# Head matmuls of an attention and feed-forward kernel: the constant 1.0 read with a step of zero in place of a tile of zeros, and fourteen of them in place of twelve

## Chip, core and metric

The kernel runs on one core of one Trainium2 chip. The metric is the device time of one execution in microseconds; the median of three runs of the kernel before is 176.75 us (176.69 to 177.01). Five engines work side by side and meet at semaphores: TensorE (PE; its weight loads have a row of their own, PEld), VectorE (DVE), ScalarE (ACT), GpSimd (POOL) and SyncE (SP), which here only issues transfers.

## What is computed

The reference is windowed attention with a few global keys and a distance bias for each head, followed by a feed-forward layer whose hidden value is the largest of three products:

```python
def _attn_ref(q, k, v, n_global, n_local):          # q, k, v: (4, 8, 768, 64)
    scores = scale * np.matmul(q, k.transpose(0, 1, 3, 2))
    rel = pos[:, None] - pos[None, :]
    is_global = pos[None, :] < int(n_global)         # 8
    is_local = (rel >= 0) & (rel < int(n_local))     # 96
    dist = np.where(is_global & ~is_local, float(n_local), np.abs(rel))
    scores = scores - slopes[:, None, None] * dist[None, :, :]
    scores = np.where(is_global | is_local, scores, -1000000000.0)
    a = np.exp(scores - np.max(scores, axis=-1, keepdims=True))
    a = a / (np.sum(a, axis=-1, keepdims=True) + 1e-09)
    return np.matmul(a, v)

def _moe_ref(x, w1, w2, w3, w_out):                  # x: (3072, 512), d_ff 768
    h = np.maximum(np.maximum(x @ w1, x @ w2), x @ w3)
    return h @ w_out
```

## The kernel before

The 3072 tokens are 24 tiles of 128 rows (four batches of six). For each pair of tiles q and k are loaded as float32, cast to bf16, transposed on TensorE into PSUM and copied to `qkT`. For each tile and each half of the heads (`u_S`) TensorE writes scores into a PSUM tile `sp`: for the first tiles it first adds the bias by two matmuls of 512 columns (L299), then the products of keys and queries (L306). ScalarE takes the exponential into `P` (L317), TensorE multiplies by v (L360), VectorE normalizes (L364 to L373), and the result is transposed into `xT`. The feed-forward layer takes chunks of 2 to 4 tiles: `u_F1` (L424) makes the hidden values, `u_F2` (L439) the output.

The order of the work is written out by hand in `SCHEDULE`: a string of units, each a letter and its numbers, issued one after the other to the engines' queues. Each engine takes its own instructions strictly in this order. The units that matter for this change are `D` (dummy matmuls), `c` (a cast of q or k), `x` (transposes with their copies), `B` and `K` (bias and mask tables of one head, made from the tile `rbq`), `S` (scores and exponentials), `C` and `W` (casts of v and of weights).

**The dummies.** `u_D(i, n)` issues n matmuls of 128x128 weights by 512 columns into a PSUM tile `wp` that nothing reads. A unit `D0.4` is `u_D(0, 4)`; a unit with n = 0 does nothing. Four dummies stand in each of D0, D4 and D5, ahead of anything else that TensorE does; D1.1 and D9.2 (three more) stand behind the first transposes, and D3.1 and D7.1 further on: 17 in all. `wp` takes a buffer of the pool `psH` with the tag "h", which has three and which the transposes' PSUM tiles use in turn, so a later dummy can wait until a copy has emptied a buffer.

**The head**, ahead of `SCHEDULE`. The first loads of k and q are issued from ScalarE's and SyncE's queues. GpSimd makes `dist` (iota, L513) and two selections of it (L520, L522) and a memset (L531) into `rbq`, then the identity `identb`. VectorE writes `shift` (L515, L516), then `zeros` (L518), the tile that the dummies read both as weights and as moving columns, then from `dist` by L524, L525, L527, L528, L529 and L530 the rest of `rbq`. ScalarE loads its table and runs one small activation (L517), and starts on the tables of `rbq` (L326 and L322) once L530 is done. On TensorE the first instruction is a dummy, which waits for the memset of `zeros`.

**The first real work on TensorE** is `x0.1.3`: the eight transposes of the first k (L282) from `qkp`, which VectorE casts (L188), and one copy to `qkT` by VectorE (L285). Then `x0.0.7`: sixteen small transposes of the first q (L261), copied by ScalarE (L268, two copies). D1.1 and D9.2 follow, then `S1.0.1`: two bias matmuls (L299) and eight products of keys and queries (L306) that need both the k copy and the q copies.

The program's preamble, ahead of all that, has GpSimd write a few constants, one value for each partition (L556 in the profile); behind it all engines meet at a barrier before their first instruction. One of these constants is 1.0 in bf16; in the kernel before nothing shown here reads it.

Of the kernel before, what the change touches and what calls it, by code (L numbers as in the profile page):

```python
# [13 lines left out]
BF16 = mybir.dt.bfloat16  # L14
# [8 lines left out]


SCHEDULE = """
    K7 l1.0 c1.0.2 K6 l1.1 B6.1 D0.4 D4.4 B5.1 D2.0 D5.4 K0 c0.1.1 c0.0.1 K2 D8.0 B0.1 B4.0 B1.0
    B3.0 x0.1.3 K1 K3 K5 c1.1.2 B7.0 x0.0.7 D1.1 D9.2 S1.0.1 Z0.1 B2.1 v0 C0.0.2 S1.1.1 G1.0 x1.0.8
    K4 M1.0 S0.0.1 M0.0 v1 x1.1.8 S2.1.1 S2.0.1 M2.0 C0.1.2 Y0.1.2 Y1.0.1 M1.1 V2.1 Y0.0.1 G2.1 A1.2
    S0.1.1 C1.0.2 C1.1.2 Y2.0.0 Y1.1.2 D3.1 S3.0.1 M3.0 M0.1 A0.2 S3.1.1 M3.1 l2.0 c2.0.2 x2.0.6
# [35 lines left out]
def kernel(  # L65
# [13 lines left out]
    nc = tc.nc  # L79
# [26 lines left out]
    persist = ctx.enter_context(tc.tile_pool(name="persist", bufs=1))  # L106
# [14 lines left out]

    identb = persist.tile([128, 128], BF16, name="identb")
    tiny = persist.tile([128, 1], FP32, name="tiny")
    zeros = persist.tile([128, 512], BF16, name="zeros")
    rbq = persist.tile([128, 3, 128], FP32, name="rbq")
    shift = persist.tile([128, 1], FP32, name="shift")
    far = persist.tile([128, 1], FP32, name="far")
# [18 lines left out]
    def heads(ap):  # L146
        return ap.rearrange("p (h e) -> p h e", e=65)
# [8 lines left out]
    def load_part(n, s):  # L156

        b, t0 = divmod(2 * n, NT)
        r = raw_pool.tile([128, 2 * DM], FP32, name="rawp", tag="raw")
        src = (q, k)[s][b, :, t0 * 128:(t0 + 2) * 128, :]  # L160
        if short_rows(n, s):
            r = r.rearrange("p (h x) -> p h x", h=H)
            dma = nc.scalar if (n, s) == (0, 1) else nc.sync
            dma.dma_start(out=r, in_=src.rearrange("h (i e) d -> i h (e d)", e=2))
        else:
            r = r.rearrange("p (z x) -> p z x", z=2)
            for z in range(2):
                nc.sync.dma_start(out=r[:, z], in_=src[4 * z:4 * z + 4].rearrange("h (i e) d -> i h (e d)", e=ET))
        raw["p", n, s] = r
# [328 lines left out]
    def u_D(i, n=0):  # L498
        if n == 0:
            return  # L500

        wp = psH.tile([128, 512], FP32, name="wp", tag="h")
        for _ in range(n):
            nc.tensor.matmul(wp, zeros[:, 0:128], zeros, start=True, stop=True)  # L504

    with tc.manual_schedule():
        load_part(0, 1)
        load_part(0, 0)

        BIGD = 60000.0  # L510
        dist = stage_pool.tile([128, 2, 2, 64], FP32, name="dist", tag="wst0")
        rtmp = stage_pool.tile([128, 128], FP32, name="rtmp", tag="wst0")
        nc.gpsimd.iota(dist, base=128, pattern=[[-1, 2], [1, 2], [2, 64]], channel_multiplier=-2,  # L513
                       allow_small_or_imprecise_dtypes=True)
        nc.vector.memset(shift[0:64], -128.0)  # L515
        nc.vector.memset(shift[64:128], -1.0)  # L516
        nc.scalar.activation(tiny, shift, AF.Exp, bias=0.0, scale=1.0)  # L517
        nc.vector.memset(zeros, 0.0)  # L518
        near, own = rbq[:, 0:2].rearrange("p s (e i) -> p s e i", e=2), rbq[:, 2]
        nc.gpsimd.affine_select(out=near, in_=dist, compare_op=ALU.is_ge, fill=BIGD, base=128,  # L520
                                pattern=[[-1, 2], [1, 2], [2, 64]], channel_multiplier=-2)
        nc.gpsimd.affine_select(out=near, in_=near, compare_op=ALU.is_ge, fill=BIGD, base=NL - 129,  # L522
                                pattern=[[1, 2], [-1, 2], [-2, 64]], channel_multiplier=2)
        nc.vector.tensor_scalar(out=own, in0=dist[:, 0].rearrange("p e i -> p (e i)"), scalar1=shift, scalar2=None, op0=ALU.add)  # L524
        nc.vector.memset(far, BIGD)  # L525
        for row in (0, 64):
            nc.vector.memset(far[row:row + NG // 2], float(NL))  # L527
        nc.vector.scalar_tensor_tensor(out=rtmp, in0=own, scalar=1.0 - NL, in1=own, op0=ALU.add, op1=ALU.mult)  # L528
        nc.vector.tensor_scalar(out=rtmp, in0=rtmp, scalar1=0.0, scalar2=far, op0=ALU.is_gt, op1=ALU.mult)  # L529
        nc.vector.scalar_tensor_tensor(out=own, in0=own, scalar=far, in1=rtmp, op0=ALU.min, op1=ALU.max)  # L530
        nc.gpsimd.memset(rbq[0:NG // 2, 0:2], float(NL))  # L531
        make_identity(nc, identb)
        for tvar in vo_first + vo_next + ve + vf:
            nc.vector.memset(heads(tvar)[:, :, 64:65], 1.0)

        units = {"l": load_part, "v": load_v, "c": cast_part, "x": u_x, "w": load_w, "o": load_wo, "C": cast_v,
                 "Y": u_Y, "Z": u_Z, "S": u_S, "M": u_M,
                 "A": u_A, "G": put_kg, "V": put_vg, "T": u_XT, "F": u_F1, "W": cast_w,
                 "K": u_K, "B": u_B, "Q": cast_wo, "O": u_F2, "E": u_E, "D": u_D}
        for u in SCHEDULE.split():  # L540
            units[u[0]](*(int(n) for n in u[1:].split(".") if n))
# [33 lines left out]
```

## Time and profile before

| | before |
|---|---|
| median of three runs | 176.75 us (176.69 to 177.01) |
| span of the profiled execution (its first to its last instruction) | 174.9 us |
| between them | 1.85 us |
| TensorE busy in the span | 169.3 us |
| VectorE, ScalarE, GpSimd busy | 132.5, 120.1, 14.3 us |
| granted TensorE clock, mean | 0.999 |

The profile is of one execution; its page gives its span, and no other time for that execution. What lies outside the span (launch, the end) is taken as the difference to the median, 1.85 us. A row of the timeline reads: start in us from the span's start, duration in us, engine, line of the kernel, operation, out<-in, shapes, how many instructions are merged; in brackets the idle time of the engine just before and what ended it. Matmuls are pipelined: each row lasts until its last result, so the durations of single matmuls overlap, and the pitch (start to start) is the cost of one in a row of them. A row of the windows gives busy time of TensorE, its weight loads, VectorE, ScalarE and GpSimd in a stretch, the granted clock, and what the transfers took and moved.

### The profile page before, as it was taken

The page shows a single profiled execution, that of the slowest core. Times are in us where ns is not written, and L with a number is a line of the kernel's source. Part 1 is how long each engine was busy: PE and PEld are TensorE (multiplying, and loading weights), DVE is VectorE, ACT ScalarE, POOL GpSimd, SP SyncE. Part 2 cuts the span into 40 slices and gives each one's busy share as a digit, 9 for nine tenths or more (in the row PEclk, how much of TensorE's full clock was granted, in tenths as well). Part 3 has the DMA queues.
Part 4 walks back from the last instruction along what each step waited for, and adds up shares of the span by engine and source line. Part 5 has one row for each costly group of instructions (what it writes and reads, how often), then busy time and mean ns, then how long its engine had stood idle before and what let it go on. Part 6 is the DMA issues. An engine that isn't in the chain of part 4 may idle for free.

```text
span 174.9 us, 4233 instructions
## 1 busy us (share of the span) xinstructions
PE 169.3 (97%) x1683; PEld 93.0 (53%) x1683; DVE 132.5 (76%) x288; ACT 120.1 (69%) x188; POOL 14.3 (8%) x25
## 2 busy tenths in 40 slices
PE   6999999999999999999999999999999999999992
PEld 2445654658684587754545545544455544444451
DVE  6668859889999999998978769995569873444510
ACT  6989999789988999999948977345594413121132
POOL 5269250000100000000000000000000000000000
PEclk9999999999999999999999999999999999999999
DMA  4999999999999999976999997563101750031205
GB/s 137 347 302 335 359 350 383 385 380 312 309 282 265 298 289 228 292 213 193 257 195 185 304 233 172 166 133 60 54 10 30 105 171 0 0 119 36 89 27 213
DMA packets 55507, 35.92 MB, mean 205 GB/s; under 512 B 18368, under 2 KB 47936, under 8 KB 55488
## 3 DMA queue, kind: packets, MB, share of 16 engines
q1 hardware_dynamic: 54304, 35.07, 73.9%
q10 hardware_dynamic: 1184, 0.59, 1.3%
q8 instruction: 13, 0.21, 0.5%
q14 instruction: 6, 0.05, 0.1%
HBM read 25.17 MB, written 6.29 MB: 180 GB/s over the span
## 4 chain that ended last, share of the span: by engine, by line
PE 94%; ACT 2%; DVE 1%; issue 1%; ACTq 0%; DVEq 0%
PE h L424 53%; PE po L439 18%; PE sp L306 7%; PE op L360 6%; PE wp L504 4%; PE tpr L261 2%; PE sp L299 2%; PE xtp L411 1%; ACT qkT L268 1%; ACT wo L496 1%; PE oph L360 1%; ACT P L317 1%; PE xtr L401 0%; PE tpp L282 0%; DVE qkT L285 0%
## 5 line engine op out<-in xcount | busy, mean ns | idle before, releaser
L424 PE MATMUL h<-xT,w 128*128 128x512 bf16 (+1 forms) x504 | 100.8, 349 | 0.0
L424 PEld LDWEIGHTS <-w 128*128 128x128 bf16 x504 | 46.7, 98 | 40.7 <-ACT w L493 0.6
L317 ACT ACTIVATE P<-sp 128x1024 bf16<-128x1024 f32 (+1 forms) x48 | 44.0, 956 | 9.2 <-PE sp L306 9.1
L429 ACT CAST h<-h 128x512 bf16<-128x512 f32 (+1 forms) x42 | 21.9, 531 | 22.1 <-PE h L424 22.1
L439 PE MATMUL po<-wo,ht 128*128 128x512 bf16 (+2 forms) x156 | 34.1, 363 | 0.0
L431 DVE TENSOR_TENSOR h<-h,h 128x512 bf16<-128x512 bf16 (+1 forms) x42 | 25.2, 605 | 10.9 <-PE h L424 8.9
L433 DVE TENSOR_TENSOR ht<-h,h 128x512 bf16<-128x512 bf16 (+1 forms) x42 | 25.5, 609 | 6.3 <-PE h L424 5.0
L334 DVE TENSOR_TENSOR P<-P,wmask 128x1024 bf16<-128x1024 bf16 x33 | 22.0, 684 | 2.0 <-ACT P L317 1.9
L439 PEld LDWEIGHTS <-ht 128*128 128x128 bf16 x156 | 14.3, 98 | 15.1 <-DVE ht L433 0.2
L448 ACT COPY ost<-po 128x512 f32<-128x512 f32 (+2 forms) x16 | 8.8, 553 | 15.8 <-PE po L439 15.3
L373 DVE TENSOR_TENSOR xb<-op,rz 128x512 bf16<-128x512 f32 x22 | 15.2, 692 | 0.8
L360 PEld LDWEIGHTS <-P 128*128 128x128 bf16 x352 | 13.4, 97 | 4.4 <-issue 0.7
L306 PE MATMUL sp<-qkT 64*128 64x128 bf16 x320 | 14.3, 218 | 0.1
L306 PEld LDWEIGHTS <-qkT 64*128 64x128 bf16 x320 | 9.3, 94 | 8.2 <-issue 5.1
L448 DVE COPY ost<-po 128x512 f32<-128x512 f32 (+1 forms) x10 | 6.5, 647 | 8.4 <-PE po L439 8.4
L188 DVE CAST qkp<-rawp 128x1024 bf16<-128x1024 f32 x12 | 8.2, 687 | 1.7 <-DMA rawp<-in_k_dram 1.6
L504 PE MATMUL wp<-zeros 128*128 128x512 bf16 x17 | 7.1, 559 | 1.5 <-DVE zeros L518 1.4
L188 ACT CAST qkp<-rawp 128x1024 bf16<-128x1024 f32 x8 | 8.4, 1050 | 0.0
L268 ACT COPY qkT<-tpr 128x512 bf16<-128x512 bf16 x12 | 6.6, 588 | 1.0 <-PE tpr L261 1.0
L268 DVE COPY qkT<-tpr 128x512 bf16<-128x512 bf16 x6 | 4.0, 688 | 3.9 <-PE tpr L261 3.9
L372 DVE RECIPROCAL rz<-op 128x8 f32<-128x8 f32 x22 | 4.4, 199 | 2.5 <-PE op L360 2.3
L360 PE MATMUL op<-vo,P 128*128 128x65 bf16 x128 | 5.4, 193 | 0.3 <-issue 0.3
(84 smaller groups left out, 127.9 us busy)
## 6 DMA issues: line engine op xcount, KB each, us to landing
rawv<-in_v_dram SPq DMA_DIRECT2D x12, 512.0 KB, 7.0
out_dram<-ost SPq DMA_DIRECT2D x23, 256.0 KB, 2.4
rawp<-in_k_dram SPq DMA_DIRECT2D x8, 512.0 KB, 5.9
rawp<-in_q_dram SPq DMA_DIRECT2D x12, 256.0 KB, 5.8
wst<-in_moe_w_dram SPq DMA_DIRECT2D x3, 1024.0 KB, 11.5
rawp<-in_q_dram SPq DMA_DIRECT2D x6, 512.0 KB, 6.2
wst<-in_moe_w_dram SPq DMA_DIRECT2D x3, 512.0 KB, 8.5
rawp<-in_k_dram SPq DMA_DIRECT2D x6, 256.0 KB, 8.6
```

The source lines that it names most:

```text
L188: copies[how](qk, src)
L306: nc.tensor.matmul(sp[:, z, i, ds], k_cols(T, hsl, jp, ds), q_cols(T, hsl, jp), start=not how, stop=True, skip_group_check=True)
L317: nc.scalar.activation(dst, src, AF.Exp, bias=0.0, scale=scale)
L334: nc.vector.tensor_mul(P, P, wmask[:, g, :, 0:2])
L360: nc.tensor.matmul(o, P[:, i, ds], vs[ds][:, h], start=(ds == 0), stop=(ds == len(vs) - 1), skip_group_check=True)
L373: nc.vector.tensor_tensor(out=x.rearrange("p (g h) d -> p g h d", g=2), in0=o4[:, :, :, 0:64], in1=rz[:, :, :, None].to_broadcast([128, 2, ...
L424: nc.tensor.matmul(ps, w123[f // 2][:, dm, j, (f % 2) * 128:(f % 2) * 128 + 128], xT[c][:, dm], start=(dm == order[0]), stop=(dm == order[ ...
L429: nc.scalar.copy(h01, ps)
L431: nc.vector.tensor_max(h01s[c, f], h01s[c, f], ps)
L433: nc.vector.tensor_max(ht[c][:, f], h01s[c, f], ps)
L439: nc.tensor.matmul(po, ht[c][:, f, tt * 128:(tt + 1) * 128], wo[:, f, cols], start=(f == 0), stop=(f == NF - 1))
L448: copy(ost, po)
```

## The change

- `zeros` is no longer allocated, and its memset on VectorE (L518) is gone.
- The dummies, all of them, read `ones`: the preamble's constant 1.0 in bf16, one element for each partition, presented as 128 x 512 with a step of zero along the columns. Both the weights and the moving columns are this view.
- D0.4 becomes D0.6: fourteen dummies ahead of the first transposes for twelve, 19 in all for 17.

```diff
-    K7 l1.0 c1.0.2 K6 l1.1 B6.1 D0.4 D4.4 B5.1 D2.0 D5.4 K0 c0.1.1 c0.0.1 K2 D8.0 B0.1 B4.0 B1.0
+    K7 l1.0 c1.0.2 K6 l1.1 B6.1 D0.6 D4.4 B5.1 D2.0 D5.4 K0 c0.1.1 c0.0.1 K2 D8.0 B0.1 B4.0 B1.0
...
-    zeros = persist.tile([128, 512], BF16, name="zeros")
+    ones = nc.const_aps.tensor(1.0, (128, 512), BF16)
...
-            nc.tensor.matmul(wp, zeros[:, 0:128], zeros, start=True, stop=True)
+            nc.tensor.matmul(wp, ones[:, 0:128], ones, start=True, stop=True)
...
-        nc.vector.memset(zeros, 0.0)
```

## The prediction

> **What bounds the kernel now.** I read the page first, then the windows by stage, then the chain of waits and the timeline of the head. The page:
>
> ```profile
> PE 169.3 (97%) x1683; PEld 93.0 (53%) x1683; DVE 132.5 (76%) x288; ACT 120.1 (69%) x188; POOL 14.3 (8%) x25
> PE 94%; ACT 2%; DVE 1%; issue 1%; ACTq 0%; DVEq 0%
> ```
>
> TensorE is busy for 97% of the span and makes 94% of the chain that ended last. The windows show where it is not (stretch and its length, busy us of PE, PEld, DVE, ACT, POOL, clock, transfers):
>
> ```profile
> 0.00:9.40 9.40, 7.85 (x43) 3.35 (x45) 6.18 (x26) 7.68 (x15) 3.30 (x11) 1.00 0.83 246
> ...
> 21.80:80.00 58.20, 58.15 (x724) 37.21 (x725) 53.59 (x119) 53.51 (x89) 3.02 (x3) 1.00 1.05 304
> 80.00:172.00 92.00, 91.49 (x691) 45.32 (x690) 62.93 (x118) 47.61 (x69) 0.00 (x0) 1.00 0.52 124
> ```
>
> From 21.8 us to 172 us TensorE idles 0.05 + 0.51 us. Whatever shifts the start of that stretch shifts the end by the same amount; nothing in it can soak up a gain or a delay. So the question is the head alone. The chain of waits through it (start, us, what):
>
> ```profile
> 1.07 0.28 DVE zeros L518
> ...
> 1.40 5.30 PE wp L504 x12
> 6.70 0.83 PE tpp L282 x8
> ...
> 7.56 0.70 DVE qkT L285
> ...
> 8.30 0.59 PE wp L504 x2
> 8.90 0.43 PE sp L299 x2
> ...
> 9.36 0.40 PE sp L306 x8
> ```
>
> Taken at its word, it says that the memset of the zeros and the dummies set the end. The timeline of TensorE and ScalarE at the same place says otherwise:
>
> ```profile
> 6.49 1.03 PE L282 MATMUL tpp<-identb,qkp 128*128 128x128 bf16 x8
> 7.45 0.41 PE L261 MATMUL tpr<-identb,qkp 64*128 64x64 bf16 x16
> 8.30 0.59 PE L504 MATMUL wp<-zeros 128*128 128x512 bf16 x2
> 8.73 0.59 PE L299 MATMUL sp<-bias,identb 128*128 128x512 bf16 x2
> 9.36 0.40 PE L306 MATMUL sp<-qkT 64*128 64x128 bf16 x8
> 3.11 2.10 ACT L326 ACTIVATE wmask<-rbq 128x384 bf16<-128x384 f32 x4 [0.43 <-DVE rbq L530]
> 5.12 1.33 ACT L322 ACTIVATE bias<-rbq 128x384 bf16<-128x384 f32 x3
> 6.36 1.59 ACT L326 ACTIVATE wmask<-rbq 128x384 bf16<-128x384 f32 x3
> 7.85 0.51 ACT L322 ACTIVATE bias<-rbq 128x384 bf16<-128x384 f32 x1
> 8.27 1.04 ACT L268 COPY qkT<-tpr 128x512 bf16<-128x512 bf16 x2
> ```
>
> Two 512-column matmuls in a row start 0.43 us apart as a pair (8.30 to 8.73), 0.215 us each. The two bias matmuls at 8.73 therefore free TensorE at 8.73 + 0.43 = 9.16, but the first products of keys and queries start at 9.36, 0.05 us after the second q copy ends on ScalarE (8.27 + 1.04 = 9.31). ScalarE has no gap back to 3.11, where it had waited for L530. **ScalarE's table work, not the dummies, releases the first products; TensorE's side has 9.36 - 9.16 = 0.20 us of slack.** The first exponential, and with it all that follows, hangs on this point.
>
> **The change, part by part.** First, when TensorE can start. The constant, and the first instructions after the preamble:
>
> ```profile
> 0.31 0.10 POOL L556 MEMSET const-bfloat16-1.0<- 128x1 bf16 x1
> 0.73 0.42 ACTq L164 DMA_DIRECT2D rawp<-in_k_dram  x1
> 0.80 0.06 DVE L515 MEMSET shift<- 64x1 f32 x1 [0.80 <-PEq L556]
> 0.83 0.36 POOL L513 IOTA dist<- 128x256 f32 x1 [0.39 <-POOLq L556]
> 1.07 0.27 DVE L518 MEMSET zeros<- 128x256 uint32 x1
> 1.40 5.30 PE L504 MATMUL wp<-zeros 128*128 128x512 bf16 x12 [1.40 <-DVE zeros L518]
> ```
>
> The constant is written by 0.41, ahead of the barrier, so a dummy has nothing left to wait for. Other engines' first instructions lie at 0.73 to 0.83; I take 0.77 for TensorE in place of 1.40, 0.63 us earlier.
>
> Second, how long the dummies hold it. Twelve run from 1.40 to the first transposes at 6.49: 5.09 us, 0.424 each, twice the 0.215 of the later pair. So TensorE is at half its pace here, and it changes between 6.49 and 8.30. (The granted clock of the first window is 1.00 and doesn't show this.) Two more cost 0.85. At this pace the fourteen end at 0.77 + 5.09 + 0.85 = 6.71, **0.22 us later than now** (0.18 to 0.28 for starts of 0.73 to 0.83): the earlier start is more than eaten by the two added. The row of the step-zero operand itself is missing from this trace. Its price lies between none, as the same shape from a full tile (0.424), and one pitch more for each matmul, if the read of one element again and again ran at half pace. I take none: the nearest row is the same matmul with another address pattern.
>
> Third, who notices 0.22 us. The data for the first transposes:
>
> ```profile
> 5.56 0.69 DVE L188 CAST qkp<-rawp 128x1024 bf16<-128x1024 f32 x1 [1.59 <-DMA rawp<-in_k_dram]
> 6.31 0.98 PEld L282 LDWEIGHTS <-qkp 128*128 128x128 bf16 x8 [0.52 <-DVE qkp L188]
> 7.02 0.35 DVE L322 TENSOR_SCALAR bias<-rbq 128x384 bf16<-128x384 f32 x1
> 7.56 0.69 DVE L285 COPY qkT<-tpp 128x1024 bf16<-128x1024 bf16 x1 [0.18 <-PE tpp L282]
> ```
>
> The cast ends at 6.25 and its weights load at 6.31, so the dummies already hold the transposes back by some 0.15 us. With 0.22 more, the k copy goes from 7.56 to 7.78, the pair of dummies that waits for its buffer from 8.30 to 8.52, the bias matmuls from 8.73 to 8.95, and TensorE is free at 9.38 for products that start at 9.36 now: the slack hides 0.20, and 0.02 us arrives. The q transposes end at 7.86 now and would at 8.08, ahead of the copy at 8.27. On VectorE the copy to `kf` and a bias table stand behind the k copy and end 0.22 later; their readers come after 9.69.
>
> The dummies may not stay at half pace until then: the pace changes with time, and work that starts 0.63 us earlier may reach the change earlier. If it falls before some 5.9 us (twelve dummies at 0.424 from 0.77 and two at 0.215 end at 6.29), the dummies are over when the cast has ended, the transposes start near 6.35 at a quarter of 0.215 each, and the k copy follows its neighbour on VectorE at 7.02 + 0.35 = 7.37, 0.19 earlier than now. Then TensorE is free for the products at 8.97, and ScalarE alone decides.
>
> The Trainium skill, page "TensorE: Matmul & The Clock Gate", Part 1, puts the change of pace at the end of a free-running window of some 3.4 us that was busy throughout. Before, that is 4.8 to 8.2 by the start at 1.40; the trace's change after 6.49 agrees. After, it would be 4.2 to 7.6, earlier than 5.9 in half of all executions.
>
> Fourth, what VectorE gains. The rows behind the memset, with GpSimd's beside them:
>
> ```profile
> 1.26 0.51 DVE L524 TENSOR_SCALAR rbq<-dist,shift 128x128 f32<-128x128 f32 x1
> 1.26 0.42 POOL L520 TENSOR_SCALAR_AFFINE_SELECT rbq<-dist 128x256 f32<-128x256 f32 x1
> 1.75 0.42 POOL L522 TENSOR_SCALAR_AFFINE_SELECT rbq<-rbq 128x256 f32<-128x256 f32 x1
> 2.00 0.31 DVE L528 SCALAR_TENSOR_TENSOR rtmp<-rbq 128x128 f32<-128x128 f32 x1
> 2.34 0.29 DVE L529 TENSOR_SCALAR rtmp<-rtmp,far 128x128 f32<-128x128 f32 x1
> ```
>
> L524 needs the iota, which ends at 0.83 + 0.36 = 1.19, and starts at 1.26 with L520, which needs it too: the memset (to 1.34) holds its start by little. But it lasts 0.51 where the same operation on the same shape, L529, lasts 0.29. So dropping the memset gives L530, and with it ScalarE's 3.11, between nothing and 0.22 us. I take 0.05: L524 ends at 1.77, 0.08 behind the end of L520 (1.68), as if it had waited for GpSimd rather than for the memset; L528 ends 0.14 behind L522.
>
> The Trainium skill, page "SBUF — State Buffer", section "Who interferes with whom", has VectorE and GpSimd share a port pair that the first to start holds to its end. By it L524 may win the pair once it is free to start a moment before L520; then L520 and L522 move back by some 0.2 us, L528 and L529 meet them instead, and the sum is again a gain of 0.05 to 0.1, no 0.22. No run here shows it yet.
>
> **The sum.** With an early change of pace: -0.05 from ScalarE's start, TensorE's side ahead of it. With a late one: +0.02. The one execution has the change 5.1 to 6.9 us behind the first dummy; as much behind 0.77 would be 5.9 to 7.7, at the border or late, but whether it follows the first dummy or the clock on the wall one trace doesn't tell. I take the early case; the other differs by 0.07 only. Between there and 21.8 us the gain could still be lost to a transfer that lands when it lands:
>
> ```profile
> 11.37 1.18 POOL L191 CAST vof<-rawv 128x512 bf16<-128x512 f32 x2 [0.77 <-DMA rawv<-in_v_dram]
> 13.86 0.33 PE L360 MATMUL oph<-vof,P 128*128 128x65 bf16 x5
> 21.64 0.26 PEld L424 LDWEIGHTS <-w 128*128 128x128 bf16 x2 [0.16 <-ACT w L493]
> ```
>
> The v cast waits for its transfer and ends at 12.55, but its reader comes at 13.86, 1.3 us later; the first weights wait for ScalarE, not for a transfer. So a small shift carries through. So I forecast 174.9 - 0.05 for the span, and with the 1.85 outside it 176.75 - 0.05 = **176.70 us**, no change that can be told. A measurement of this kernel tells about 0.2% from no change, 0.35 us.
>
> **The rivals.**
>
> *ScalarE's start moves in full.* If all that VectorE's steps lose to GpSimd goes, ScalarE could start when its first small activation is done (2.68) instead of 3.11; TensorE's side allows 9.36 - 8.97 = 0.39. That is the most the head can give: 176.36. For it: L524's 0.51 against 0.29. Against: the steps wait on GpSimd's, which do not get shorter.
>
> *TensorE doesn't start earlier.* The change then does not do what it says: something other than the memset (the load of its own instructions, the barrier) holds TensorE to its old start. The products come at its start + 5.94 for the fourteen + 2.67 (6.49 to 9.16), later than 9.36 if the start is later than 0.75, and over 0.35 us later from a start of 1.10. At 1.40 it costs 0.85 - 0.20 = 0.65: 177.40. Against: the wait named in the row at 1.40 is the memset's.
>
> *The pace falls back.* If the pace changes as early as 4.2, the dummies end at about 5.5 and TensorE idles until 6.3. If it then drops to half once more for as long as it takes to recover (some 3 us of matmuls from 9.4, less what hides under ScalarE), it costs about 1.5 us: 178.2. Against: idle stretches of 0.4 us at 8.3 and 9.3 leave the later pace alone, though they are shorter.
>
> *Step zero reads at half pace.* Fourteen dummies of 0.85 last 11.9 us, the transposes start at 12.7 for 6.49, less 0.20: 176.75 + 6.0 = 182.7. Nothing in the trace speaks for or against it.
>
> **How the numbers follow.** The forecast (with 0.02 late as its other half) 0.56, ScalarE's start in full 0.24, TensorE not earlier 0.12, the pace falls back 0.05, half pace reads 0.03. The forecast's own range is 176.5 to 176.95, its two ends with the spread of the three runs. To hold eight in ten I go down to the bound of the first rival, 176.3, and up to 177.1, half of the second rival; the slow two and the rest of the second stay out. Faster by over 0.35: 0.24. Slower: the two slow ones and the second rival's larger half with some room, 0.08 + 0.09 = 0.17. Within: 0.59.
>
> **What would show it.** In the profile after: the first dummy at 0.73 to 0.83 in place of 1.40 (else the second rival); fourteen at 0.424 up to 6.7, or at 0.215 from some point on; the first products within 0.1 us of 9.36 with the q copies of ScalarE ending just ahead of them; ScalarE's first table row at 3.0 to 3.11; the first L424 within 0.1 us of 21.81. A first L424 over 0.35 us off either way, or TensorE idle time after 21.8 that differs by that much, would make the prediction wrong, and ScalarE's q copies ending well ahead of the first products would make its central step wrong.

## The result, and the profile after

| | before | after |
|---|---|---|
| median | 176.75 us (176.61 to 177.12, 11 runs) | 176.28 us (176.20 to 176.69, 11 runs) |
| ratio, 95% interval | | 0.9976 (0.9968 to 0.9985) |
| span of the profiled execution | 174.9 us | 174.9 us |
| first L306 (products of keys and queries) | 9.36 us | 9.36 us |
| first L424 (feed-forward) | 21.81 us | 21.56 us |

The changed kernel is faster by 0.24% of 176.75, 0.42 us (0.27 to 0.57 by the interval). The forecast was 176.70 and no change that can be told; the measured time lies at the lower edge of its range (176.3). The profiled execution of the changed kernel happens to be the slowest of its eleven (176.69 us), so its span shows no gain; the profile of a second set of runs, further down, shows an ordinary one.

The line numbers behind L517 are one lower than before. The page after, its busy times and its chain:

```profile
PE 168.4 (96%) x1664; PEld 92.8 (53%) x1685; DVE 133.0 (76%) x287; ACT 120.1 (69%) x188; POOL 14.0 (8%) x25
...
PE 88%; ACT 5%; DVE 3%; issue 2%; POOL 1%; POOLq 0%; ACTq 0%
```

The page has 1664 matmuls beside 1685 weight loads, where before had 1683 of each: 21 matmul records are missing from this trace. So its busy time of TensorE and TensorE's 88% of the chain are too low and can't be held against the 169.3 us and 94% of before; starts of rows can be compared.

The timeline of the head after, TensorE, VectorE, GpSimd and ScalarE in turn:

```profile
0.77 5.71 PE L504 MATMUL wp<-const-bfloat16-1.0 128*128 128x512 bf16 x14 [0.77 <-PEq L555]
8.70 0.59 PE L299 MATMUL sp<-bias,identb 128*128 128x512 bf16 x2
9.36 0.40 PE L306 MATMUL sp<-qkT 64*128 64x128 bf16 x8
1.22 0.54 DVE L523 TENSOR_SCALAR rbq<-dist,shift 128x128 f32<-128x128 f32 x1 [0.27 <-POOL dist L513]
1.26 0.42 POOL L519 TENSOR_SCALAR_AFFINE_SELECT rbq<-dist 128x256 f32<-128x256 f32 x1
3.11 2.09 ACT L326 ACTIVATE wmask<-rbq 128x384 bf16<-128x384 f32 x4 [0.43 <-DVE rbq L529]
8.26 1.04 ACT L268 COPY qkT<-tpr 128x512 bf16<-128x512 bf16 x2
```

TensorE starts at 0.77, released by the barrier alone. The operation behind the memset (L523) starts at 1.22 in place of 1.26 and lasts 0.54 in place of 0.51: it ends at 1.76 in place of 1.77. ScalarE starts its tables at 3.11, as before, ends its q copies at 9.30, and the first products start at 9.36, as before. **In the head nothing is gained and nothing lost.** Still the first feed-forward matmul comes earlier, so the gain lies between 9.4 and 21.8 us. The later rows of the same execution, weight loads, TensorE and ScalarE:

```profile
18.55 0.54 PEld L360 LDWEIGHTS <-P 128*128 128x128 bf16 x16 [0.22 <-ACT P L317]
19.37 0.29 PEld L261 LDWEIGHTS <-qkp 64*128 64x128 bf16 x16 [0.28 <-POOL qkp L188]
21.56 0.81 PE L424 MATMUL h<-xT,w 128*128 128x512 bf16 x2
26.69 1.04 ACT L493 CAST w<-wst 128x1024 bf16<-128x1024 f32 x1 [1.03 <-DMA wst<-in_moe_w_dram]
```

And the same weight loads before, which the prediction did not show:

```profile
18.55 0.47 PEld L360 LDWEIGHTS <-P 128*128 128x128 bf16 x14 [0.21 <-ACT P L317]
19.45 0.12 PEld L360 LDWEIGHTS <-P 128*128 128x128 bf16 x2 [0.42 <-issue]
19.62 0.17 PEld L261 LDWEIGHTS <-qkp 64*128 64x128 bf16 x8
```

Weight loads (PEld) are compared here because none of their records is missing. Before, a group of sixteen weight loads that starts at 18.55 is cut in two: fourteen, then 0.42 us in which TensorE waits for nothing that the profile shows ("issue"), then two. After, all sixteen run at a stretch. What this execution still loses at 19.37 it loses to a cast on GpSimd, and at 26.69 ScalarE waits 1.03 us for a weight transfer; before, the same cast of weights is earlier:

```profile
26.36 1.05 ACT L493 CAST w<-wst 128x1024 bf16<-128x1024 f32 x1 [0.45 <-DMA wst<-in_moe_w_dram]
```

The weight loads that need this cast wait for it:

```profile
27.79 0.11 PEld L424 LDWEIGHTS <-w 128*128 128x128 bf16 x2 [0.48 <-ACT w L493]
```

Compared load by load with before, this execution is 0.25 us ahead up to there, 0.08 behind that wait, and at 50.2, at a wait for VectorE (L373), nothing is left. So it gave 0.17 of its 0.25 us back to a transfer that landed late, and the rest later.

### The profile page after: what moved, and what is told of

Read it like the earlier page. It is cut to its first block, busy times and chain, and to the rows that moved or that the text cites. A ratio compares the mean times of both kernels' runs of the same rounds, so it can differ in the third digit from the quotient of the medians.

```text
span 174.9 us, 4215 instructions
## 1 busy us (share of the span) xinstructions
PE 168.4 (96%) x1664; PEld 92.8 (53%) x1685; DVE 133.0 (76%) x287; ACT 120.1 (69%) x188; POOL 14.0 (8%) x25
## 4 chain that ended last, share of the span: by engine, by line
PE 88%; ACT 5%; DVE 3%; issue 2%; POOL 1%; POOLq 0%; ACTq 0%
PE h L424 52%; PE po L439 18%; PE sp L306 7%; PE op L360 5%; ACT wmask L326 2%; PE tpr L261 2%; PE sp L299 2%; ACT bias L322 1%; ACT qkT L268 1%; PE xtp L411 1%; ACT P L317 1%; POOL qkp L188 1%; PE oph L360 1%; PE xtr L401 0%; DVE xb L373 0%
## 5 line engine op out<-in xcount | busy, mean ns | idle before, releaser
L424 PE MATMUL h<-xT,w 128*128 128x512 bf16 (+1 forms) x489 | 99.5, 348 | 0.9 <-issue 0.3
L424 PEld LDWEIGHTS <-w 128*128 128x128 bf16 x504 | 46.6, 98 | 41.0 <-ACT w L493 1.1
L429 ACT CAST h<-h 128x512 bf16<-128x512 f32 (+1 forms) x42 | 21.8, 531 | 21.9 <-PE h L424 21.8
L373 DVE TENSOR_TENSOR xb<-op,rz 128x512 bf16<-128x512 f32 x22 | 15.2, 692 | 0.8
L306 PE MATMUL sp<-qkT 64*128 64x128 bf16 x320 | 14.3, 217 | 0.2
L306 PEld LDWEIGHTS <-qkT 64*128 64x128 bf16 x320 | 9.3, 94 | 8.4 <-issue 5.1
L504 PE MATMUL wp<-const-bfloat16-1.0 128*128 128x512 bf16 x19 | 7.5, 539 | 0.9 <-PEq L555 0.8
L261 PE MATMUL tpr<-identb,qkp 64*128 64x64 bf16 x208 | 5.4, 190 | 0.6 <-DVE qkp L188 0.2
L493 ACT CAST w<-wst 128x1024 bf16<-128x1024 f32 x5 | 5.1, 1047 | 1.0 <-DMA wst<-in_moe_w_dram 1.0
## 6 DMA issues: line engine op xcount, KB each, us to landing
wst<-in_moe_w_dram SPq DMA_DIRECT2D x3, 1024.0 KB, 11.6
```

The source lines that it names most:

```text
L306: nc.tensor.matmul(sp[:, z, i, ds], k_cols(T, hsl, jp, ds), q_cols(T, hsl, jp), start=not how, stop=True, skip_group_check=True)
L373: nc.vector.tensor_tensor(out=x.rearrange("p (g h) d -> p g h d", g=2), in0=o4[:, :, :, 0:64], in1=rz[:, :, :, None].to_broadcast([128, 2, ...
L424: nc.tensor.matmul(ps, w123[f // 2][:, dm, j, (f % 2) * 128:(f % 2) * 128 + 128], xT[c][:, dm], start=(dm == order[0]), stop=(dm == order[ ...
L429: nc.scalar.copy(h01, ps)
```

## The experiments

Four theories stand in the expectations. A: TensorE's own instructions arrive late at 18.9 us, and a few instructions more shift when they are brought in. B: the gain comes from the head, by the earlier start or the pace. C: what decides lies ahead of D9.2 (and, in its first form, has to be full-length dummies). D: chance of where the program's pieces are placed. All dummies write `wp`, which nothing reads, so none of the edits but the last changes what is computed on the way, and the last only the order.

**The whole in one table.** "Transfer" is the first transfer of queue q8 (below). "Packets ahead" counts, in the trace, how many of the 512 packets of 1 KB that load the first feed-forward weights had started before it. "Stall" goes from the start of the 222nd weight load to the start of the 223rd, which without a stall are 0.03 us apart.

| run | first L306 | stall of the weight loads | transfer | packets ahead | first L424 | median us | ratio (95%) |
|---|---|---|---|---|---|---|---|
| before | 9.36 | 18.93 to 19.45 | 16.93 to 18.01 | 479 | 21.81 | 176.75 | |
| after | 9.36 | none | 15.83 to 17.02 | 95 | 21.56 | 176.28 | 0.9976 (0.9968 to 0.9985) |
| e1, changed kernel again | 9.36 | none | 15.40 to 16.59 | 9 | 21.34 | 176.20 | 0.997 (0.996 to 0.998) |
| e2, ones, 12 | 9.36 | 18.93 to 19.64 | 17.20 to 18.25 | 499 | 22.00 | 176.84 | 1.0004 (0.9995 to 1.0013) |
| e3, zeros, 14 | 9.37 | none | 15.81 to 16.95 | 146 | 21.35 | 176.19 | 0.9971 (0.9960 to 0.9982) |
| e4, zeros, 12 + 2 short | 9.37 | 18.88 to 19.61 | 17.10 to 18.22 | 503 | 22.04 | 176.78 | 1.0002 (0.9994 to 1.0011) |
| e5, zeros, 14, two fewer in D9 | 9.36 | none | 15.89 to 17.02 | 146 | 21.34 | 176.26 | 0.9984 (0.9967 to 1.0000) |
| e6, zeros, 12, 2 short behind D9 | 9.36 | 18.87 to 19.41 | 16.93 to 18.07 | 502 | 21.84 | 176.77 | 0.9998 (0.9988 to 1.0007) |
| e7, zeros, 12 + 4 short | 9.36 | none | 15.37 to 16.52 | 25 | 21.33 | 176.19 | 0.9963 (0.9949 to 0.9977) |
| e8, zeros, 13 | 9.36 | 18.90 to 19.37 | 16.97 to 18.09 | 491 | 21.76 | 176.72 | 0.9992 (0.9983 to 1.0001) |
| e9, zeros, 12, 4 short behind D9 | 9.36 | 18.81 to 19.50 | 16.99 to 18.12 | 490 | 21.99 | 176.87 | 1.0002 (0.9993 to 1.0011) |
| e10, memset of 1.0 | 9.37 | 18.94 to 19.53 | 17.05 to 18.19 | 499 | 21.89 | 176.75 | 0.9994 (0.9983 to 1.0004) |
| e11, ones, 12 + 4 short | 9.36 | none | 15.75 to 16.84 | 99 | 21.34 | 176.19 | 0.9967 (0.9954 to 0.9979) |
| e12, changed kernel, B7.0 later | 8.99 | 18.54 to 19.06 | 16.39 to 17.48 | 323 | 21.48 | 176.34 | 0.9976 (0.9966 to 0.9987) |

### The two parts apart: e1 to e4

e1 is the changed kernel again, with no edit. Expected:

> The changed kernel unchanged, for a second profile. Theory A (instruction supply): the gain is the 0.46 us stall of TensorE at 18.96 us in the profile of before, which ends 1.4 us after a 16 KB instruction transfer; four more TensorE instructions ahead of it bring that transfer forward (15.83 for 16.93 us in the first profile of after) and the stall goes. It expects about 176.3 us, no stall near 19 us, and the first L424 some 0.4 us ahead of 21.81. Theory B (head): the earlier change of TensorE's pace brings the first products of keys and queries forward, to about 9.0 us; it expects 176.3 us with L306 starting 0.3 to 0.4 us ahead of 9.36.

Its timeline, TensorE, ScalarE and TensorE again:

```profile
0.77 4.60 PE L504 MATMUL wp<-const-bfloat16-1.0 128*128 128x512 bf16 x14 [0.77 <-PEq L555]
6.42 0.62 PE L282 MATMUL tpp<-identb,qkp 128*128 128x128 bf16 x8 [1.04 <-DVE qkp L188]
8.28 1.03 ACT L268 COPY qkT<-tpr 128x512 bf16<-128x512 bf16 x2
9.36 0.40 PE L306 MATMUL sp<-qkT 64*128 64x128 bf16 x8 [0.21 <-ACT qkT L268]
21.34 1.02 PE L424 MATMUL h<-xT,w 128*128 128x512 bf16 x3
```

This trace, too, lacks 21 matmul records. In this execution the pace changed early: the fourteen dummies take 4.60 us in place of 5.71, and TensorE then idles 1.04 us for the k cast. The products start at 9.36 all the same, and now the row itself names the q copies as their releaser, with 0.21 us of idle TensorE ahead of them. The chain of waits from 18.5 to 21.8, before:

```profile
18.55 0.60 PE op L360 x14
19.15 0.30 issue
19.45 0.24 PE op L360 x2
19.69 0.34 PE tpr L261 x16
...
21.81 0.38 PE h L424
```

and in e1:

```profile
18.56 0.66 PE op L360 x16
19.22 0.34 PE tpr L261 x16
...
21.34 0.38 PE h L424
```

Up to 18.56 the two agree to 0.01 us; at the transposes (L261) they are 19.69 - 19.22 = 0.47 us apart, and at L424 21.81 - 21.34 = 0.47 still. The whole lead is made in this one place. (0.14 us of it is lost again at 50.2, at the wait for L373; this profiled execution took 176.39 us, the median of its run is 176.20.)

e2 is the changed kernel with twelve dummies ahead, so the constant alone:

```diff
-... B6.1 D0.6 D4.4 ...
+... B6.1 D0.4 D4.4 ...
```

> Constant 1.0 as operand, no memset, but twelve dummies: TensorE starts early, with as many instructions as before. Theory A: the stall near 19 us is back, 176.7 us (within 0.15 of before). Theory B: the dummies end by 5.9 us at the latest, so the products come as early as in the changed kernel or earlier: 176.2 to 176.3 us.

e3 is the kernel before with fourteen, so the count alone:

```diff
-... B6.1 D0.4 D4.4 ...
+... B6.1 D0.6 D4.4 ...
```

> The zeros and their memset stay, fourteen dummies: TensorE starts at 1.40, with four more instructions. Theory A: the stall near 19 us goes, but the dummies last 0.4 to 0.85 us longer and 0.2 to 0.65 of it reaches the first products: 176.4 to 177.0 us, with no stall of 0.46 at 19 us. Theory B: 176.9 to 177.4 us, and the stall there as before.

Their weight loads, e2 first:

```profile
18.56 0.48 PEld L360 LDWEIGHTS <-P 128*128 128x128 bf16 x14 [0.22 <-ACT P L317]
19.64 0.11 PEld L360 LDWEIGHTS <-P 128*128 128x128 bf16 x2 [0.61 <-issue]
```

```profile
18.56 0.54 PEld L360 LDWEIGHTS <-P 128*128 128x128 bf16 x16 [0.22 <-ACT P L317]
19.15 0.29 PEld L261 LDWEIGHTS <-qkp 64*128 64x128 bf16 x16
```

The constant with twelve dummies is as slow as before (176.84) and stalls; the zeros with fourteen, with TensorE's start still at 1.40, are as fast as the changed kernel (176.19) and don't. That is below the 176.4 to 177.0 that A had for e3: the longer dummies cost nothing at the products (9.37); in this execution the pace changed within them, at 5.58. **The part of the change that pays is the two more dummies, not the constant, the memset or the earlier start.** B falls with this.

e4 is the kernel before with two very short matmuls, four instructions, behind the dummies of D0:

```diff
     for _ in range(n):
         nc.tensor.matmul(wp, zeros[:, 0:128], zeros, start=True, stop=True)
+    if i == 0:
+        for _ in range(2):
+            nc.tensor.matmul(wp[:, 0:8], zeros[:, 0:128], zeros[:, 0:8], start=True, stop=True)
```

> The kernel before with two matmuls of 8 columns more (four TensorE instructions with their weight loads) in D0: same start, same length of the dummies within 0.1 us, only the position of everything behind in the instruction stream is moved by four. Theory A: 176.3 us, like the changed kernel, and no stall near 19 us. Theory B: 176.75 us, no change.

It is a miss for A in its simplest form: as many instructions as in e3, and yet slow (176.78), with the stall.

```profile
18.56 0.41 PEld L360 LDWEIGHTS <-P 128*128 128x128 bf16 x12 [0.22 <-ACT P L317]
19.61 0.18 PEld L360 LDWEIGHTS <-P 128*128 128x128 bf16 x4 [0.64 <-issue]
```

But these rows tell what the stall is. Two loads more in the stream, and it comes two loads earlier, behind the twelfth of the sixteen.

### Where the stall sits, and what ends it: e5 to e8

e5 takes two dummies away again behind the first transposes, so that all later instructions stand where they stood before:

```diff
-... B6.1 D0.4 D4.4 ... D1.1 D9.2 ...
+... B6.1 D0.6 D4.4 ... D1.1 D9.0 ...
```

> Zeros, fourteen dummies ahead of the first transposes, but D9.2 left out, so that from there on every TensorE instruction stands where it stood before the change. Theory A (position: the stall at 18.9 us hangs on where the stream of TensorE's instructions is cut into 16 KB pieces): stall back, 176.7 to 176.8 us. Theory C (what counts is that the fourteen dummies last full length, by what they change in the head, not the position behind them): 176.2 us, no stall.

It is fast by its median (176.26), without the stall, a second miss for A, which had the stall back. Three of its ten executions took 177.1 to 177.2, which widens its interval to 1.0000; the profile is of one that took 176.27, and what the three lost their 0.9 us to isn't known.

e6 puts the two short matmuls of e4 behind D9 (`if i == 9:`):

> The kernel before with two matmuls of 8 columns more behind D9's two dummies: four instructions more only from 8.7 us on. Theory A: 176.2 us, no stall at 18.9 us (the pad in D0 should then have done it too, and did not). Theory C: 176.75 us, stall as before.

e7 is e4 with four short ones (`range(4)`):

> The kernel before with four matmuls of 8 columns more in D0, eight TensorE instructions. Theory A with another cut than thought: eight instructions do what four of this kind did not, 176.2 to 176.3 us and no stall. Theory C: 176.75 us.

e8 is the kernel before with thirteen dummies (`D0.5`):

> Zeros, thirteen dummies: two instructions more and half the added length. Theory A: either 176.2 us or 176.75 us, nothing between, by which side of the cut two instructions fall. Theory C: between, or like before. Both: the time goes with the presence of the stall at 18.9 us and nothing else.

e6 and e8 are slow and stall; e7 is fast and doesn't. So full-length dummies are not needed, which ends C's first form. The weight loads of e8:

```profile
18.55 0.45 PEld L360 LDWEIGHTS <-P 128*128 128x128 bf16 x13 [0.22 <-ACT P L317]
19.37 0.14 PEld L360 LDWEIGHTS <-P 128*128 128x128 bf16 x3 [0.37 <-issue]
```

Thirteen dummies, thirteen of sixteen loads ahead of the stall; twelve and two short ones, twelve; twelve dummies, fourteen. Counted from the start of the program, the stall is behind the 222nd weight load in all eight profiles that have it. It is tied to a place in TensorE's instruction stream, not to a place in the computation.

What is late at that place is shown by the queues. On the page before:

```profile
q8 instruction: 13, 0.21, 0.5%
```

Thirteen transfers of 0.21 / 13 = 0.016 MB bring in instructions. Only TensorE has enough of them: 1683 matmuls and 1683 weight loads make 259 for each transfer, where VectorE has 288 in all. And they follow TensorE's count: in all fourteen profiles the second of them starts after 279 to 283 weight loads and the last after 1613 to 1617. The first starts after 144 to 152 in the profiles without the stall and after 162 to 184 in those with it. The transfers from 16.35 to 17.3 us before hold the first of them:

```profile
q1 hardware_dynamic: 289, 0.33, 108.3%
q8 instruction: 1, 0.02, 7.1%
```

and in e1 it is in the stretch from 15 to 16.35 us:

```profile
q1 hardware_dynamic: 548, 0.42, 109.7%
q8 instruction: 1, 0.02, 5.5%
```

In both the 16 transfer engines are full with data (108% and 110% by this count). The table holds the rest. In each stalled run TensorE goes on 1.28 us (e8, 18.09 to 19.37) to 1.58 us (e12, 17.48 to 19.06) behind the end of this transfer (1.44 before, 1.39 in e2 and e4, 1.34 in e6 and e10). In the runs without it the transfer ends at 16.52 to 17.02, so the same wait is over by 17.02 + 1.58 = 18.60 at the latest, ahead of the 18.8 to 19.0 where the 223rd weight load starts. Stall and time go together in all fourteen profiles: e12 apart, the kernels with it take 176.72 to 176.87, those without it 176.19 to 176.28.

### Ahead of D9 or behind it, and the value in the tile: e9 to e11

e9 puts four short matmuls behind D9 (`if i == 9:`, `range(4)`), which e7 had ahead:

> The kernel before with four matmuls of 8 columns more behind D9's two dummies: eight TensorE instructions more from 8.7 us on, nothing changed ahead of that. Theory A (position in the stream, with eight instructions enough in any place ahead of 11 us): 176.2 us, the instruction transfer starts at 15.3 to 15.9 us, no stall at 18.9. Theory C (what decides lies ahead of D9): 176.75 us, transfer near 17 us, stall as before.

It is slow (176.87), with the stall, now behind ten of the sixteen loads, 14 - 4:

```profile
18.55 0.35 PEld L360 LDWEIGHTS <-P 128*128 128x128 bf16 x10 [0.21 <-ACT P L317]
19.50 0.24 PEld L360 LDWEIGHTS <-P 128*128 128x128 bf16 x6 [0.59 <-issue]
```

e10 fills the tile of the kernel before with 1.0, an edit that leaves every instruction at its place in the order:

```diff
-        nc.vector.memset(zeros, 0.0)
+        nc.vector.memset(zeros, 1.0)
```

> The kernel before with 1.0 in place of 0.0 written into the tile that the dummies read: the same instructions in the same places, but another program. Theory A and C: 176.75 us, stall as before. Theory D (chance: where a program lies in memory decides whether its instruction transfer is early): as likely 176.2 us without the stall as 176.75 us with it. It also tells whether ones in place of zeros as data matter: they should not.

It is as before in its median (176.75; ratio 0.9994), with the stall, so the value that the dummies read makes no difference that can be told. Two of its ten executions took 176.33 and 176.35, below the lowest of before in that set (176.54); no profile of them is kept. The edit does move TensorE's start, from 1.40 to 1.67, because this memset is longer:

```profile
1.12 0.48 DVE L518 MEMSET zeros<- 128x512 bf16 x1 [0.17 <-DVE shift L516]
1.53 0.24 DVE L524 TENSOR_SCALAR rbq<-dist,shift 128x128 f32<-128x128 f32 x1
```

The products start at 9.37 even so.

e11 is e2 with the four short ones of e7:

```diff
-... B6.1 D0.6 D4.4 ...
+... B6.1 D0.4 D4.4 ...
...
     for _ in range(n):
         nc.tensor.matmul(wp, ones[:, 0:128], ones, start=True, stop=True)
+    if i == 0:
+        for _ in range(4):
+            nc.tensor.matmul(wp[:, 0:8], ones[:, 0:128], ones[:, 0:8], start=True, stop=True)
```

> The changed kernel with twelve dummies of 512 columns and four of 8 in place of fourteen: the early start of the run with twelve ones (which had the stall and 176.84 us), and eight instructions more than that. Theory A: 176.2 us, no stall. Theory C, if only full-length dummies count: 176.8 us with the stall. It can only beat the changed kernel if the first products come ahead of 9.36, which no run so far shows.

It is fast (176.19). Four short matmuls ahead of the first transposes do the same to the kernel with the constant and to the one with the zeros; behind D9 they do nothing. C holds in this form, but it doesn't give the number: e4, with two short ones there, stays slow, and e3, with as many instructions there, is fast. D isn't excluded: e4 and the two short executions of e10 would fit it.

### Making the head earlier: e12

If ScalarE's tables release the first products, as the prediction said, then moving one of them behind the q copies must bring the products forward. e12 is the changed kernel with one unit moved:

```diff
-... K5 c1.1.2 B7.0 x0.0.7 D1.1 ...
+... K5 c1.1.2 x0.0.7 B7.0 D1.1 ...
```

> The changed kernel with one of ScalarE's bias tables (B7.0, 0.41 us of ScalarE) moved behind the two q copies of x0.0.7; it is read only by the second half of the heads. The same TensorE stream. If ScalarE's table work releases the first products (the prediction's central step), they come 0.2 to 0.3 us ahead of 9.36, as far as TensorE's own chain lets them (the bias matmuls end near 9.1), and the time falls by as much: 175.9 to 176.1 us, unless the later start of the instruction transfer brings the stall at 18.9 back (then 176.5). If the dummies or TensorE's chain release them, 9.36 stays and the time is that of the changed kernel, 176.2 to 176.3 us.

Its timeline, ScalarE and TensorE in the order of time, then the weight loads:

```profile
7.84 1.05 ACT L268 COPY qkT<-tpr 128x512 bf16<-128x512 bf16 x2
8.79 0.53 ACT L322 ACTIVATE bias<-rbq 128x384 bf16<-128x384 f32 x1
8.99 0.40 PE L306 MATMUL sp<-qkT 64*128 64x128 bf16 x8
...
18.22 0.42 PEld L360 LDWEIGHTS <-P 128*128 128x128 bf16 x12 [0.22 <-ACT P L317]
19.06 0.17 PEld L360 LDWEIGHTS <-P 128*128 128x128 bf16 x4 [0.43 <-issue]
```

The products start at 8.99, 0.37 us earlier than in any other run, and the lead is still there at the weight loads (18.22 for 18.55 in e1, 0.33). Then the stall is back, and the first L424 comes at 21.48, 0.14 later than in e1. The time, 176.34 us, is the changed kernel's (ratios 0.9976 and 0.9976), between the 175.9 to 176.1 that were expected without the stall and the 176.5 with it. What the head gained here was eaten by the wait for instructions. No run beats the changed kernel by more than its interval: e3, e7 and e11 have 176.19 to its 176.20 in e1.

## Where the prediction was right and where it was wrong

The forecast, 176.70 us and no change that can be told, missed a gain of 0.42 us (0.27 to 0.57) that can be told. The time lies below the forecast's own range, 176.5 to 176.95, and 0.02 us below 176.3, the lower end of the wide one. That it comes so near is luck: this end was set for ScalarE's start in full, and that did not happen.

**ScalarE's tables, not the dummies, release the first products**: right. The first products are at 9.36 or 9.37 in every run but e12, with TensorE's start at 0.77, 1.40 or 1.67 and with the dummies ending early or late; e1's row names the q copies, and e12 moved the products by moving a table.

**TensorE starts at 0.77**: right, 0.77 (forecast 0.73 to 0.83). The rival by which it would not start earlier falls. Its price falls too: e3 has fourteen dummies from 1.40, and the products start at 9.37, where the rival had them 0.65 us later.

**Fourteen dummies at 0.424, step zero at no price**: right. In the trace they start 0.427 us apart from the constant, as they do from the zeros. Half-pace reads fall. The pace changed at another moment in each execution, so both halves of the forecast occurred (dummies lasting 5.71 us in one, 4.60 in the other), and neither arrived at the products. The rival "the pace falls back" had its condition in e1, a TensorE idle for 1.04 us from 5.4, and did not happen: the eight transposes behind it took 0.62 us, and the time of this execution was 176.39.

**VectorE gains 0.05**: mis-sized, it is 0.01 for L523's end, and ScalarE's 3.11 doesn't move. The operation waits for the iota now (its row says 0.27 us of idle time, released by GpSimd), and before, the memset held it only 0.04 us longer. In e10 the same operation starts at 1.53, lasts 0.24 and ends at 1.77 again: its end doesn't follow its own start, and comes 0.08 to 0.09 behind the end of GpSimd's selection (1.26 + 0.42 = 1.68) in all three. The port pair of the Trainium skill, page "SBUF — State Buffer", section "Who interferes with whom", would have given 0.05 to 0.1 here by the prediction's estimate; in these rows L523 starts 0.04 ahead of GpSimd's L519, which still starts at 1.26 and lasts 0.42 as before, so the trace doesn't show that the first to start wins. The rival with ScalarE's start in full, which named a size near the measured one (176.36), falls with it: the size was near by luck and the mechanism wrong.

**"The first exponential, and with it all that follows, hangs on this point"**, and with it "so the question is the head alone" and "so a small shift carries through": **this is the step that failed.** The first L424 does not hang on 9.36 alone. Between the two lies a second wait, at 18.93 to 19.45, that belongs to the instruction stream and not to the data; the change removed it without moving 9.36 at all, and in e12 it swallowed 0.33 us that did carry through up to 18.2. (That is against e1. Against before, which has the stall too, e12's 0.33 carry through.) The prediction read the windows from 21.8 on and the chain up to 9.4, and took what lies between for a chain that hands shifts on. The chain of before had the row that said otherwise, "0.30 issue" at 19.15. The prediction passed over it. Its own sign of being wrong, a first L424 over 0.35 us from 21.81, is not in the profile after (0.25 earlier) but in e1 (0.47 earlier).

**"Nothing in it can soak up a gain or a delay"**, of the stretch from 21.8 to 172 us: wrong in part. The profiled execution of the changed kernel lost its 0.25 us there, at 27.8 and 50.2, and e1 lost 0.14 of 0.47 at 50.2; e3 and e12 carried theirs to the end (0.45 of 0.47 and 0.32 of 0.33).

The cost of two dummies was counted in time on TensorE (0.85 us of which 0.02 arrives). What they also change, when the next instructions are brought in, was not counted at all.

**What stays open.** That the wait ends with the late transfer is read from fourteen profiles; no run could move that transfer by itself. Why two full dummies or four short matmuls ahead of the first transposes make it start earlier, and one full, two short, or any behind D9 don't, isn't settled. What can be told is the shape: it starts early, after 9 to 146 of the 512 packets of the first feed-forward weights, or late, after 479 to 503 of them, and with e12 once in between (323). That is as if it were asked for shortly before or after TensorE's wait for a later unit's transposes at 11.2 to 11.6 us, while those packets are put into the queues (SyncE's issue, 10.62 to 11.73 before). This is argued and not shown, and the counts speak against it: by that wait TensorE has begun 84 weight loads in e4 and e6 and 86 in e9, which are late, and 82 in e5, which is early. A trial with that weight load moved elsewhere was not made.

## What to carry to other kernels

In the chain of waits, a piece called "issue" of some tenths of a microsecond on the engine that sets the end is a wait like any other: look whether it stays at the same count of instructions when a few are put ahead of it, and whether an instruction transfer lands shortly before it ends. Where it does, test the two parts of a change apart before you credit its purpose; here the part that was meant to cost paid, and the part that was meant to pay did nothing. A head made earlier is worth only what the next such wait lets through.

## What the runs showed of the hardware

- TensorE's weight loads stood 0.47 to 0.73 us apart (e8, e4; 0.03 without the stall) at one place in its instruction stream when the first transfer of instructions ran late among full data queues, and went on 1.28 to 1.58 us behind its landing. The Trainium skill, page "Runtime: NRT & Kernel Launch", section "Instruction fetch mechanics", has such a refill "mostly hidden". For the later twelve of this kernel the trace agrees: from 21.8 to 172 us TensorE idles 0.56 us in all before. For the first the trace disagrees, and it is 0.3% of the time.
- The matmul from one element with a step of zero, as weights and as moving columns, has the pitch of a full tile: 0.427 us at half pace as from the zeros, 0.218 at full pace (e1; 0.216 from the zeros, e3).
- TensorE's pace doubled 2.9 us behind its first matmul in e1 (3.68 by the starts of the dummies, from 0.77), and 4.2 us behind it in e3 (5.58, from 1.40). The Trainium skill, page "TensorE: Matmul & The Clock Gate", Part 1, states about 3.4 us, give or take half a microsecond. e1 lies at that edge, e3 beyond it, and before further still: there the transposes that end the row at 6.49 (from 1.40) still run at half pace, over 5 us behind the first matmul. The measurement decides: here the moment varied by more than that half microsecond.
